# Which pairs of hidden chunks use seven half products, and where the factors of x are made

## The chip, the cores and the metric

The kernel runs on one core of a Trainium2 chip. The metric is the device time of one execution in microseconds (us); lower is better. The engines are TensorE (PE, with its weight loads PEld), VectorE (DVE), ScalarE (ACT), GpSimd (POOL) and SyncE (SP, which issues the DMAs).

## The reference, cut to what matters

```python
x = attention(q, k, v)                  # chunks of 64, as 2304 tokens x 512
x = (x @ w_a) * (x @ w_b) @ w_out       # 512 -> 1536 -> 512
p = probs / probs.sum(-1)
for e in range(4):                      # 512 -> 1024 -> 512
    out += p[:, e:e+1] * (relu(x @ w1[e]) @ w2[e])
```

The change is in the second line. Everything is float32, and each product is made as three matmuls of a value cut into a high and a low part: high by low, high by high, low by high.

## The kernel before, in words

**Tiles.** The 2304 tokens are 18 tiles of 128, in blocks 0 (256 tokens) and 1 to 4 (512 tokens each). The 1536 hidden columns are 12 chunks of 128, in six pairs F = 0 to 5. For a chunk and a block there are a = x @ w_a and b = x @ w_b (12 matmuls each), their product, and the output product, which adds into the accumulator of the block.

**Two forms.** In the plain form (`ab_steps`, L478) a chunk and a block take eight steps of three matmuls. After the last one DVE multiplies (L502), ACT writes the high part (L94, to `gh`), and POOL the low part (L109, to `ag`). The output product (`x2_steps`, L510) of a block and a pair is four steps of six matmuls (three for each chunk; lines L445 to L447), and each ends with an addition to the accumulator (`xacc`, by ACT for pair 0, else by DVE). It is put between steps of the next block: the list `after` says behind which.
In the other form (`seq_ab`, L727) blocks 1 and 2 are made together with a pair of chunks by two sequences of seven half products in place of eight (L614; six matmuls at L605 each). It needs sums of the weights, S1 to S4 (`sums`, L268: four DVE subtractions or additions of 256 columns; `ent_s`, L272, called twice per sequence: a high part on ACT, a low part on POOL, tile `S`), and four factors of x, T1 to T4, which are differences of x's blocks 1 and 2. `first_combos` (L666) makes the factors in 16 steps: `whole` (L675) adds a high and a low part again, `minus` (L695) subtracts, and a split makes a high part on ACT and a low part on POOL or DVE (tile `cT`, at L109 and L101). T1 takes the place of a part of block 2's x, so it can only be made when no plain product of block 2 follows.

**Weights.** A pair has six pieces: a of both chunks, b of both, out of both. `begin_f32` (L263) takes one from 64-bit to 32-bit floats: two ACT operations (L144, L145), three of DVE (L146, L147, L150), one of POOL (L158), then the DMA of a later piece. `prep_end` (L254) splits it: high on ACT, low on POOL (tile `w`).

**Order.** All engines work through their instructions in the order in which the program writes them. That order is written out by hand: `put(u, s, ...)` sets an operation behind step s of block u (in pair 0: behind step s of span u of the list `spans`; "A" is `seq_ab`). Pair 0 runs beside the attention, and its spans 9 and 10 are block 4. Then pair 1 runs blocks 3, 4, 0 and then "A"; pairs 2 to 4 run 4, "A", 3, 0; pair 5 runs "A", 3, 4, 0. The second layer (L830, with half products too) follows and takes the rest of the time.

Of the kernel before, what the change touches and what calls it, by code (L numbers as in the profile page):

```python
# [28 lines left out]
def fused_kernel(  # L29
# [29 lines left out]
    NP1 = w1p.shape[0] // 2  # L59
# [107 lines left out]
    def split_w(src, t=None):  # L167
        t = w_tile() if t is None else t
        split_hi(t[:, 0, :], src)
        sub_hi(nc.gpsimd, t[:, 1, :], src, t[:, 0, :])  # L170
        return t
# [37 lines left out]
    def w_sums(a11, a12, a21, a22):  # L209

        s23 = cv_p.tile([P, 512], F32, tag="t", name="s23", bufs=4)
        s14 = cv_p.tile([P, 512], F32, tag="t", name="s14", bufs=4)
        s2, s3 = s23[:, :256], s23[:, 256:]
        s1, s4 = s14[:, :256], s14[:, 256:]
        add_sb(s1, a21, a22)
        add_sb(s3, a11, a21, ALU.subtract)
        add_sb(s2, s1, a11, ALU.subtract)
        add_sb(s4, a12, s2, ALU.subtract)
        return s23, s14
# [28 lines left out]
    def prep_begin(n=1):  # L248
        for _ in range(n):
            key = pieces[nxt["begin"]]  # L250
            nxt["begin"] += 1
            ready[key] = from_f64(raws[key].pop(0))
# [10 lines left out]
    def begin_f32(F, i):  # L263

        prep_begin()
        f32s[F, i] = ready[0, 2 * F + i % 2, i // 2]

    def sums(F, m):  # L268
        a1, a2 = f32s[F, 2 * m], f32s[F, 2 * m + 1]
        f32s[F, "s", m] = w_sums(a1[:, :256], a1[:, 256:], a2[:, :256], a2[:, 256:])  # L270

    def ent_s(F, m, i):  # L272

        t = late["mid"].tile([P, 2, 512], F32R, tag="S", name="S", bufs=2)
        split_w(f32s[F, "s", m][i], t)
        for x, name in enumerate((("S2", "S3"), ("S1", "S4"))[i]):
            wts["s", F, m, name] = tuple(t[:, h, 256 * x : 256 * x + 256] for h in range(2))
# [313 lines left out]
    def in_place(x1, x2):  # L591
        q = quarters(x1, x2)
        return combos(*q, (q[0], q[1], q[2], q[2]))

    def in_turn(c):
        s1, s2, s3 = c["sums"]
        return c["first"] + s1 + c["T3"] + s2 + c["T2"] + s3 + c["T1"] + c["T4"] + c["B22"]
# [250 lines left out]
    with tc.manual_schedule():  # L848
# [55 lines left out]
        def put(u, s, *go):  # L904
            T.setdefault((u, s), []).extend(go)
# [1 line left out]
        put(6, 3, lambda: begin_f32(1, 0))  # L907
        put(6, 6, prep_end)
        put(7, 3, lambda: begin_f32(1, 1))
        put(8, 7, lambda: sums(1, 0))  # L910
        put(9, 1, lambda: begin_f32(1, 2))
        put(9, 4, prep_end)
        put(9, 5, lambda: ent_s(1, 0, 0))
        put(9, 7, lambda: ent_s(1, 0, 1))
        put(10, 1, prep_end)
        put(10, 2, lambda: begin_f32(1, 3))
        put(10, 6, lambda: sums(1, 1))
        cx = first_combos()
        for i in (5, 7):
            put(10, i, cx.pop(0))  # L920
        x2 = []
        for r, (f, j, i0, nt) in enumerate(spans):
            steps = list(ab_steps(f, j, i0, nt))
# [22 lines left out]
        for F in range(1, NP1):  # L946
            T = {}
            end = F == NP1 - 1
            if F == 1:
                put(3, 8, prep_end)  # L950
                put(3, 9, lambda: begin_f32(F, 4))
                put(3, 10, lambda: begin_f32(F, 5))
                put(3, 13, prep_end)
                put(3, 15, prep_end)
                at = [(3, 5), (3, 11), (3, 13), (4, 1), (4, 3), (4, 4), (4, 6), (4, 8), (4, 10), (4, 12)]
                at += [(4, 14), (0, 2), (0, 5), (0, 7)]
                for (u, s), go in zip(at, cx, strict=True):
                    put(u, s, go)
            else:
                if F == 2:  # L960
                    put(4, 0, lambda: begin_f32(F, 3))
                    put(4, 1, prep_end)
                    put(4, 3, lambda: ent_s(F, 0, 0))
                    put(4, 5, prep_end)
                    put(4, 7, lambda: ent_s(F, 0, 1))
                    put(4, 8, lambda: sums(F, 1))
                    put(4, 9, lambda: begin_f32(F, 4))
                    put(4, 11, lambda: begin_f32(F, 5))
                    put(4, 13, prep_end)
                    put("A", 0, prep_end)  # L970
                else:
                    u = "A" if end else 4
                    put(u, 0, lambda: begin_f32(F, 4))
                    put(u, 8 if end else 2, lambda: begin_f32(F, 5))
                    put(u, 3, prep_end)
                    put(u, 10, prep_end)
            put("A", 4, lambda: ent_s(F, 1, 0))
            put("A", 7, lambda: ent_s(F, 1, 1))
            if not end:
                n = F + 1  # L980
            if F == 1:
                put("A", 6, lambda: begin_f32(n, 0))
                put("A", 8, lambda: begin_f32(n, 1), prep_end)
                put("A", 11, prep_end)
                put("A", 13, lambda: sums(n, 0), lambda: begin_f32(n, 2))
            elif not end:
                put("A", 6, lambda: begin_f32(n, 0))
                put("A", 8, lambda: begin_f32(n, 1))
                put("A", 10, prep_end)
                put(3, 0, lambda: sums(n, 0))  # L990
                put(3, 3, lambda: ent_s(n, 0, 0))
                put(3, 5, lambda: ent_s(n, 0, 1))
                put(3, 14, lambda: begin_f32(n, 2))
                put(0, 4, prep_end)
                put(0, 6, lambda: begin_f32(n, 3))
                put(0, 8, prep_end)
                put(0, 11, lambda: sums(n, 1))
                put(0, 12, prep_end)
            else:
                w_next = w2_steps(0, True)  # L1000
                for u, s in ((4, 3), (0, 4), (0, 8), (0, 12)):
                    put(u, s, lambda: w_next.pop(0)())
                at = [(3, 11 + i) for i in range(4)] + [(3, 15), (4, 0), (4, 2), (4, 4), (4, 6)]
                at += [(4, 8), (4, 10), (4, 12), (4, 14), (4, 15)] + [(0, 2 * i + 1) for i in range(4)]
            for j in ("A", 3, 4, 0) if end else (3, 4, 0, "A") if F == 1 else (4, "A", 3, 0):
                if j == "A":
                    steps = seq_ab(F)
                    after = [4, 5, 6, 7]
                else:
                    nt = blocks[j][1]  # L1010
                    s0, s1 = (list(ab_steps(f, j, 0, nt)) for f in (2 * F, 2 * F + 1))
                    steps = s0[:4] + s1[:4] + s0[4:] + s1[4:]
                    if len(x2) > 4:
                        after = [6 + i for i in range(8)]
                    elif j == 0:
                        after = [8 + 2 * i for i in range(4)]
                    elif (F, j) == (1, 3):
                        after = [4 + i for i in range(4)]
                    else:
                        after = [5 + i for i in range(4)]  # L1020
                if end and j == 3:
                    place = dict(B11="s1", B21="s2", T3="s3", T2="s4", T1="s5", T4="s6", B22="s7")
                    for (u, s), go in zip(at, in_turn(in_place(acc[1], acc[2])), strict=True):
                        put(u, s, go)
                for s, step in enumerate(steps):
                    step()
                    for i, go in enumerate(x2):
                        if after[i] == s:
                            go()
                    for go in T.get((j, s), ()):  # L1030
                        go()
                fs = (2 * F, 2 * F + 1)
                x2 = [x for i in ((1, 2) if j == "A" else (j,)) for x in x2_steps(fs, i, 0, blocks[i][1])]
                if end and j == "A":
                    mid.close()
                    late["p"] = ctx.enter_context(tc.tile_pool(name="late", bufs=1))
# [3 lines left out]
        for p, (j1, j2) in enumerate(((1, 2), (3, 4))):  # L1040
            for g in range(NG2):
                end = p == 1 and g == NG2 - 1
# [97 lines left out]
```

## Time and profile before

| | us |
|---|---|
| runs before | 1270.72, 1270.89, 1272.07 |
| median | 1270.89 |
| the profiled execution | 1272.2 |
| its span, first to last instruction | 1270.4 |

1.8 us of the profiled execution lie around its span. Busy shares are of the span. A matmul's record lasts longer than the time until the next one starts, since matmuls overlap; the time that one takes of the whole is from start to start.

### The profile page before, as it was taken

To read this page: it belongs to the slowest core of one execution; us is meant where nothing else is said; L and a number is where in the kernel's file an instruction comes from. 1 tells how busy PE (TensorE), PEld (TensorE's weight loads), DVE (VectorE), ACT (ScalarE), POOL (GpSimd) and SP (SyncE) were. 2 spreads that over 40 slices of the span, in tenths; PEclk is the share of its full clock that TensorE was granted. 3 is DMA by queue.
4 is the path that set the end of the run, shared out by engine and by line. 5 is a ranking of instruction groups with operands and counts; after the bars stand their busy time and mean duration, and the time that the engine had idled before them with its cause. 6 is when DMAs were issued, how large, how long until landed. Compare 5 with 4: busy or idle time off the path is not lost.

```text
span 1270.4 us, 17613 instructions
## 1 busy us (share of the span) xinstructions
PE 1244.1 (98%) x6856; PEld 1035.2 (81%) x6856; DVE 776.5 (61%) x1233; ACT 451.4 (36%) x746; POOL 374.3 (29%) x290
## 2 busy tenths in 40 slices
PE   8999889899999999999999999999999999999998
PEld 5887768688888888888888888888888888888887
DVE  7865366666665665666566555665575555555555
ACT  4644332423323332322222222222264444444442
POOL 4523544645434553533332323223230000000000
PEclk9999989999999999999999999999999999999999
DMA  7621111212111110234544354534575454544443
GB/s 255 233 90 42 34 33 34 67 34 67 34 34 51 33 50 1 100 134 152 196 156 160 133 189 159 182 133 147 217 249 166 152 163 150 164 152 148 166 133 132
DMA packets 48035, 156.37 MB, mean 123 GB/s; under 512 B 5456, under 2 KB 5456, under 8 KB 47952
## 3 DMA queue, kind: packets, MB, share of 16 engines
q1 hardware_dynamic: 47952, 155.25, 36.7%
q8 instruction: 54, 0.88, 0.3%
q14 instruction: 29, 0.24, 0.1%
HBM read 100.18 MB, written 55.05 MB: 122 GB/s over the span
## 4 chain that ended last, share of the span: by engine, by line
PE 86%; DVE 6%; issue 2%; ACT 2%; POOL 2%; DMA 1%; SPq 0%; POOLq 0%; DVEq 0%; ACTq 0%
PE ps L830 29%; PE pm L605 28%; PE pm L492 11%; PE ps L445 5%; PE ps L447 5%; PE ps L446 5%; PE ps L605 2%; DMA kept<-kept 1%; POOL w L109 1%; PE ps L391 1%; DVE s L101 1%; DVE d L326 1%; DVE mx L325 1%; DVE t L147 1%; POOL ag L109 1%
## 5 line engine op out<-in xcount | busy, mean ns | idle before, releaser
L830 PE MATMUL ps<-w,h 128*128 128x512 f32 x1536 | 353.4, 389 | 0.0
L830 PEld LDWEIGHTS ps<-w,h 128*128 128x128 f32 x1536 | 288.3, 188 | 59.7
L817 DVE SCALAR_TENSOR_TENSOR oacc<-ps,pr,oacc 128x512 f32<-128x512 f32 x270 | 191.7, 749 | 104.4 <-PE ps L830 104.4
L605 PE MATMUL pm<-cT,w 128*128 128x512 f32 x768 | 184.9, 389 | 0.0
L605 PE MATMUL pm<-cB,w 128*128 128x512 f32 x696 | 177.6, 390 | 2.3 <-ACT ag L630 2.0
L605 PEld LDWEIGHTS pm<-cT,w 128*128 128x128 f32 x768 | 144.0, 188 | 29.8
L605 PEld LDWEIGHTS pm<-cB,w 128*128 128x128 f32 x696 | 129.1, 188 | 29.2 <-ACT ag L630 2.9
L109 POOL TENSOR_TENSOR w<-raw,w 128x512 fp32r<-128x512 f32 x64 | 82.7, 1293 | 206.1 <-ACT w L94 142.2
L492 PE MATMUL pm<-xh,w 128*128 128x512 f32 (+1 forms) x576 | 137.2, 359 | 2.8 <-ACT w L94 2.8
L198 ACT CAST w<-kept 128x1024 fp32r<-128x1024 f32 x96 | 99.0, 1046 | 58.9 <-DMA kept<-kept 57.6
L492 PEld LDWEIGHTS pm<-xh,w 128*128 128x128 f32 x576 | 100.3, 192 | 19.9 <-ACT w L94 3.2
L97 DVE TENSOR_TENSOR xacc<-ps,xacc 128x512 f32<-128x512 f32 (+1 forms) x112 | 69.5, 631 | 73.4 <-PE ps L447 73.0
L109 POOL TENSOR_TENSOR ag<-ag,gh 128x512 fp32r<-128x512 f32 (+1 forms) x61 | 78.1, 1286 | 123.1 <-ACT gh L94 121.7
L445 PE MATMUL ps<-ag,w 128*128 128x512 f32 (+1 forms) x244 | 91.8, 376 | 8.9 <-POOL ag L109 8.5
L94 ACT CAST gh<-ag 128x512 fp32r<-128x512 f32 (+1 forms) x61 | 34.9, 572 | 179.5 <-DVE ag L97 143.5
L447 PE MATMUL ps<-gh,w 128*128 128x512 f32 (+1 forms) x244 | 90.8, 372 | 2.3 <-POOL w L109 2.3
L446 PE MATMUL ps<-gh,w 128*128 128x512 f32 (+1 forms) x244 | 90.7, 372 | 0.0
L158 POOL TENSOR_TENSOR t<-t,raw 128x512 int32<-128x512 int32 x36 | 48.0, 1332 | 94.5 <-PE ps L445 31.7
L492 PE MATMUL pm<-xl,w 128*128 128x512 f32 (+1 forms) x288 | 71.8, 361 | 1.4 <-DVE xl L101 1.4
L109 POOL TENSOR_TENSOR w<-s,w 128x512 fp32r<-128x512 f32 x32 | 43.7, 1385 | 72.9 <-ACT w L94 72.9
L97 DVE TENSOR_TENSOR ag<-pm,ag 128x512 f32<-128x512 f32 (+1 forms) x61 | 38.2, 626 | 42.1 <-PE pm L492 26.4
L445 PEld LDWEIGHTS ps<-ag,w 128*128 128x128 f32 x244 | 46.9, 192 | 20.0 <-POOL ag L109 11.1
(122 smaller groups left out, 1686.1 us busy)
## 6 DMA issues: line engine op xcount, KB each, us to landing
kept<-w SPq DMA_DIRECT2D x96, 512.0 KB, 6.1
kept<-kept SPq DMA_DIRECT2D x96, 512.0 KB, 3.3
raw<-in_w1p_dram SPq DMA_DIRECT2D x36, 512.0 KB, 3.6
raw<-in_w2p_dram SPq DMA_DIRECT2D x32, 512.0 KB, 4.5
q<-in_q_dram SPq DMA_DIRECT2D x18, 256.0 KB, 4.5
k<-in_k_dram SPq DMA_DIRECT2D x18, 256.0 KB, 4.7
v<-in_v_dram SPq DMA_DIRECT2D x18, 256.0 KB, 4.5
out_dram<-oacc SPq DMA_DIRECT2D x18, 256.0 KB, 2.6
```

The costliest lines, as they stand in the source:

```text
L94: nc.scalar.copy(out=dst, in_=src)
L97: nc.vector.tensor_tensor(out=out, in0=in0, in1=in1, op=op)
L109: eng.tensor_tensor(out=dst, in0=src, in1=hi.bitcast(F32), op=ALU.subtract)
L158: nc.gpsimd.tensor_tensor(out=t.bitcast(I32), in0=t.bitcast(I32), in1=low.bitcast(I32), op=ALU.add)
L198: nc.scalar.copy(out=t, in_=fetched.pop(key))
L445: nc.tensor.matmul(out=ps[:, :n], lhsT=wh, rhs=al, start=(m == 0), stop=False)
L446: nc.tensor.matmul(out=ps[:, :n], lhsT=wh, rhs=ah, start=False, stop=False)
L447: nc.tensor.matmul(out=ps[:, :n], lhsT=wl, rhs=ah, start=False, stop=(m == last))
L492: nc.tensor.matmul(out=st[i][:, :n], lhsT=x, rhs=y, start=m == 0, stop=m == 3 * KD - 1)
L605: nc.tensor.matmul(out=ps, lhsT=x, rhs=y, start=first and kk == 0 and m == 0, stop=kk == 1 and m == 2, skip_group_check=not first,)
L817: nc.vector.scalar_tensor_tensor(out=o, in0=ps, scalar=p1, in1=o, op0=ALU.mult, op1=ALU.add)
L830: nc.tensor.matmul(out=ps[k], lhsT=x[:, s], rhs=y, start=f == 0 and m == 0, stop=f == 1 and m == 2,)
```

## The change

Pair 1 makes blocks 1 and 2 in the plain form, in the order 1, 2, 3, 4, 0, and has no "A". So the weight sums of pair 1 (`sums(1, ...)`, `ent_s(1, ...)`) are gone, and the 16 steps of the factors, of which two stood in the last span of pair 0 and 14 in blocks 3, 4 and 0 of pair 1, stand in blocks 2, 3, 4 and at the start of block 0, one at a time. The weights of pair 2 are begun in blocks 4 and 0 of pair 1 and no longer in its "A". In pairs 2 to 4 the output product of block 0 of the pair before stands three steps later in block 4, and the out weights are begun and split later; `sums(F, 1)` moves from block 0 of the pair before to step 2 of block 4, but for pair 5.

```diff
         put(7, 3, lambda: begin_f32(1, 1))
-        put(8, 7, lambda: sums(1, 0))
         put(9, 1, lambda: begin_f32(1, 2))
         put(9, 4, prep_end)
-        put(9, 5, lambda: ent_s(1, 0, 0))
-        put(9, 7, lambda: ent_s(1, 0, 1))
         put(10, 1, prep_end)
         put(10, 2, lambda: begin_f32(1, 3))
-        put(10, 6, lambda: sums(1, 1))
-        cx = first_combos()
-        for i in (5, 7):
-            put(10, i, cx.pop(0))
...
             if F == 1:
-                put(3, 8, prep_end)
-                put(3, 9, lambda: begin_f32(F, 4))
-                put(3, 10, lambda: begin_f32(F, 5))
-                put(3, 13, prep_end)
-                put(3, 15, prep_end)
-                at = [(3, 5), (3, 11), (3, 13), (4, 1), (4, 3), (4, 4), (4, 6), (4, 8), (4, 10), (4, 12)]
-                at += [(4, 14), (0, 2), (0, 5), (0, 7)]
-                for (u, s), go in zip(at, cx, strict=True):
+                put(1, 8, prep_end)
+                put(1, 9, lambda: begin_f32(F, 4))
+                put(1, 10, lambda: begin_f32(F, 5))
+                put(1, 13, prep_end)
+                put(1, 15, prep_end)
+                at = [(2, 0), (2, 3), (2, 8), (2, 11), (2, 14), (3, 0), (3, 4), (3, 6), (3, 9), (3, 12)]
+                at += [(3, 14), (4, 3), (4, 5), (4, 11), (4, 14), (0, 1)]
+                for (u, s), go in zip(at, first_combos(), strict=True):
                     put(u, s, go)
             else:
-                if F == 2:
-                    put(4, 0, lambda: begin_f32(F, 3))
-                    put(4, 1, prep_end)
-                    put(4, 3, lambda: ent_s(F, 0, 0))
-                    put(4, 5, prep_end)
-                    put(4, 7, lambda: ent_s(F, 0, 1))
-                    put(4, 8, lambda: sums(F, 1))
-                    put(4, 9, lambda: begin_f32(F, 4))
-                    put(4, 11, lambda: begin_f32(F, 5))
-                    put(4, 13, prep_end)
-                    put("A", 0, prep_end)
-                else:
-                    u = "A" if end else 4
-                    put(u, 0, lambda: begin_f32(F, 4))
-                    put(u, 8 if end else 2, lambda: begin_f32(F, 5))
-                    put(u, 3, prep_end)
-                    put(u, 10, prep_end)
-            put("A", 4, lambda: ent_s(F, 1, 0))
-            put("A", 7, lambda: ent_s(F, 1, 1))
+                u = "A" if end else 4
+                if not end:
+                    put(4, 2, lambda: sums(F, 1))
+                put(u, 0 if end else 4, lambda: begin_f32(F, 4))
+                put(u, 8 if end else 6, lambda: begin_f32(F, 5))
+                put(u, 3 if end else 8, prep_end)
+                put(u, 10 if end else 13, prep_end)
+                put("A", 4, lambda: ent_s(F, 1, 0))
+                put("A", 7, lambda: ent_s(F, 1, 1))
...
             if F == 1:
-                put("A", 6, lambda: begin_f32(n, 0))
-                put("A", 8, lambda: begin_f32(n, 1), prep_end)
-                put("A", 11, prep_end)
-                put("A", 13, lambda: sums(n, 0), lambda: begin_f32(n, 2))
+                put(4, 1, lambda: begin_f32(n, 0))
+                put(4, 7, lambda: begin_f32(n, 1))
+                put(4, 9, prep_end)
+                put(4, 13, lambda: sums(n, 0))
+                put(4, 15, lambda: ent_s(n, 0, 0))
+                put(0, 2, lambda: ent_s(n, 0, 1))
+                put(0, 3, lambda: begin_f32(n, 2))
...
+            if not end:
                 put(0, 4, prep_end)
                 put(0, 6, lambda: begin_f32(n, 3))
                 put(0, 8, prep_end)
-                put(0, 11, lambda: sums(n, 1))
+                if n == NP1 - 1:
+                    put(0, 11, lambda: sums(n, 1))
                 put(0, 12, prep_end)
...
-            for j in ("A", 3, 4, 0) if end else (3, 4, 0, "A") if F == 1 else (4, "A", 3, 0):
+            for j in ("A", 3, 4, 0) if end else (1, 2, 3, 4, 0) if F == 1 else (4, "A", 3, 0):
...
-                    elif (F, j) == (1, 3):
+                    elif F > 1 and j == 4 and not end:
+                        after = [8 + i for i in range(4)]
+                    elif j == 1:
                         after = [4 + i for i in range(4)]
```

## Rows read from the trace of the kernel before

**Rows 1.** The page: busy time of each engine over the span.
```profile
PE 1244.1 (98%) x6856; PEld 1035.2 (81%) x6856; DVE 776.5 (61%) x1233; ACT 451.4 (36%) x746; POOL 374.3 (29%) x290
```
**Rows 2.** What TensorE waited for: total us, times, longest us.
```profile
PE ps L445 <- POOL ag L109: 8.5, 5, 3.7
PE pm L492 <- ACT w L94: 2.8, 1, 2.8
PE ps L447 <- POOL w L109: 2.3, 2, 1.5
```
**Rows 3.** Pairs 1, 2, 3: length, busy PE, PEld, DVE, ACT, POOL, clock, DMA, GB/s.
```profile
137.10:218.40 81.30, 71.79 (x326) 58.63 (x325) 43.59 (x59) 24.64 (x45) 35.22 (x25) 0.94 0.11 32
218.40:304.20 85.80, 81.38 (x373) 67.50 (x372) 58.32 (x83) 28.17 (x51) 47.88 (x36) 0.98 0.17 51
304.20:375.50 71.30, 71.15 (x347) 59.91 (x346) 43.99 (x67) 22.55 (x41) 33.59 (x27) 1.00 0.15 44
```
**Rows 4.** Timeline of TensorE: start, us, matmuls, [idle before <- releaser].
```profile
122.70 0.50 PE L445 MATMUL ps<-ag,w 128*128 128x512 f32 x1 [0.88 <-POOL ag L109]
...
145.08 0.71 PE L445 MATMUL ps<-ag,w 128*128 128x512 f32 x1 [3.71 <-POOL ag L109]
...
148.83 0.40 PE L445 MATMUL ps<-ag,w 128*128 128x512 f32 x1
...
160.89 1.98 PE L492 MATMUL pm<-xh,w 128*128 128x512 f32 x8
162.70 0.61 PE L492 MATMUL pm<-xl,w 128*128 128x512 f32 x2
...
164.69 0.50 PE L447 MATMUL ps<-gh,w 128*128 128x512 f32 x1 [0.84 <-POOL w L109]
168.09 0.50 PE L445 MATMUL ps<-ag,w 128*128 128x512 f32 x1 [2.91 <-POOL ag L109]
...
170.30 0.80 PE L447 MATMUL ps<-gh,w 128*128 128x512 f32 x1 [1.47 <-POOL w L109]
...
175.98 0.40 PE L445 MATMUL ps<-ag,w 128*128 128x512 f32 x1
...
188.85 0.50 PE L445 MATMUL ps<-ag,w 128*128 128x512 f32 x1 [0.58 <-POOL ag L109]
...
229.47 0.96 PE L492 MATMUL pm<-xh,w 128*128 128x512 f32 x3 [2.81 <-ACT w L94]
...
233.87 0.43 PE L445 MATMUL ps<-ag,w 128*128 128x512 f32 x1
...
249.30 1.65 PE L605 MATMUL pm<-cB,w 128*128 128x512 f32 x6 [1.61 <-ACT ag L630]
```
**Rows 5.** Timeline of GpSimd around the first two boundaries of pair 1.
```profile
138.62 2.40 POOL L677 TENSOR_TENSOR tmp<-cB 128x1024 f32<-128x1024 f32 x1
...
160.40 1.31 POOL L158 TENSOR_TENSOR t<-t,raw 128x512 int32<-128x512 int32 x1 [1.24 <-DVE t L150]
161.66 1.30 POOL L109 TENSOR_TENSOR ag<-ag,gh 128x512 fp32r<-128x512 f32 x1
163.07 1.56 POOL L109 TENSOR_TENSOR w<-t,w 128x512 fp32r<-128x512 f32 x1
```
**Rows 6.** Timeline of VectorE, alone and at the same two boundaries.
```profile
120.43 0.76 DVE L101 SCALAR_TENSOR_TENSOR s<-t 128x256 f32<-128x256 f32 x2
...
138.70 2.94 DVE L101 SCALAR_TENSOR_TENSOR s<-t 128x256 f32<-128x256 f32 x2 [1.57 <-POOL t L158]
...
160.09 0.69 DVE L97 TENSOR_TENSOR ag<-pm,ag 128x512 f32<-128x512 f32 x1
161.98 3.20 DVE L101 SCALAR_TENSOR_TENSOR cT<-tmp,cT 128x512 fp32r<-128x512 f32 x2 [1.21 <-ACT cT L94]
165.11 0.68 DVE L97 TENSOR_TENSOR ag<-pm,ag 128x512 f32<-128x512 f32 x1
```
**Rows 7.** Timeline of ScalarE at the second boundary.
```profile
160.81 0.62 ACT L94 CAST gh<-ag 128x512 fp32r<-128x512 f32 x1 [3.21 <-DVE ag L97]
```

More of the change, by code (lines that the diff above doesn't have):

```diff
@@ L996, in fused_kernel @@
                 put(0, 8, prep_end)
-                put(0, 11, lambda: sums(n, 1))
+                if n == NP1 - 1:
+                    put(0, 11, lambda: sums(n, 1))
                 put(0, 12, prep_end)
-            else:
+            if end:
                 w_next = w2_steps(0, True)
```

## The prediction

> **What bounds the kernel now.** The page first: TensorE is busy for 1244.1 of 1270.4 us [rows 1], and no other engine comes near. So a change pays either by fewer matmuls or by taking a wait of TensorE away. This one adds matmuls; the question is which waits it takes. The table of waits names them: TensorE waits for low parts that POOL makes of the gated product (8.5 us) and of weights (2.3), and for a weight's high part (2.8) [rows 2]. The stretches tell where: pair 1 has 71.79 busy us in 81.30 at a granted clock of 0.94, pair 2 has 81.38 in 85.80 at 0.98, pair 3 has 71.15 in 71.30 at 1.00 [rows 3]. So the waits, and the clock's falls behind them, lie in pairs 1 and 2, which the change rewrites, and pair 3 shows the same kind of work without any.
>
> **The waits priced.** Undisturbed, eight matmuls of 512 columns take 162.70 - 160.89 = 1.81 us, 0.227 each [rows 4]. A wait costs 0.16 more than its bracket (a matmul's own 0.39 outlasts the 0.227 by that), and the first matmul behind it some 0.11 more (0.50 for 0.39). I name them by place.
> - A, output products of block 3 in the last spans of pair 0: 0.88 + 0.27 = 1.15.
> - B, output product of block 4 in pair 1's first block: 3.71 + 0.16, and then nine matmuls from 145.08 to 148.83 take 3.75 instead of 9 x 0.227 = 2.04, at the lower of the two clock levels (1.2 for 2.4 GHz): 5.58.
> - C, the next boundary: 0.84 + 2.91 + 1.47 + 3 x 0.16, and 13 matmuls from 170.30 to 175.98 take 5.68 for 2.95: 8.43, with two slow first matmuls 8.7.
> - D, into block 0: 0.58 + 0.27 = 0.85.
> - E, pair 2's block 4 for the split of its second a piece: 2.81 + 0.16, and 12 matmuls from 229.47 to 233.87 take 4.40 for 2.72: 4.65.
> - F, in pair 2's "A": 1.61 + 0.27 = 1.88.
> Together 22.8 us [rows 4].
>
> **What is added.** Two blocks times two chunks times 24 matmuls are 96; the two sequences have 84. So 12 more, 12 x 0.227 = 2.72 us, with nothing to hide them. Everything else of TensorE's work stays.
>
> **What is removed or moved, by its place.**
> *Last spans of pair 0 and B.* B's chain: the sums of the second two pieces stand on DVE ahead of the last product. Two of their four operations took 2.94 us, where a pair alone takes 0.76 [rows 6], beside a `whole` on POOL of 2.40 [rows 5]. Sums, `whole` and weight parts leave this place. DVE, ACT and POOL then need 0.69, 0.62 and 1.30 [rows 5 to 7] behind the last matmul, 2.6 us and small hand-overs; the second chunk's low part is wanted five steps (15 x 0.227 = 3.4) and three matmuls later, at 4.1. B goes to 0. A has the same chain of 2.6 with the same two steps before it; it loses at most its lengthened POOL operation: 1.05 stays.
> *C.* Now the first boundary inside pair 1 is from block 1 to block 2, with the same conversions of the two out pieces at the same steps (8, 9, 10, 13, 15), but without factor steps between. Up to the product of the first chunk nothing changes: DVE at 160.09 [rows 6], ACT at 160.81 [rows 7], POOL at 161.66, since POOL's conversion of the second out piece ran from 160.40 [rows 5]. What goes is T3 on DVE (3.20 for two), which held the second chunk's product back from 160.8 to 165.11 [rows 6]. POOL then works through its queue at 1.30 each: first low part until 162.96, first out weight until 164.3, second low part until 165.6, second out weight until 166.9. TensorE wants them at 162.70 + 2 x 0.227 = 163.15 [rows 4], 163.6, 163.8 and 164.3: it waits some 0.7, 1.0 and 0.9, in all 2.6 us instead of the 5.7 before. Does the clock fall? Bounds: 0, as at F, whose single 1.61 us left it high, and 2.7, as at C now. The longest single piece is like F, the sum like E, where 1.7 was lost. I take 1.4, near E, since over half of that stretch is idle.
> *Blocks 2 to 4.* Two `whole` (2.40 each [rows 5]) queue on POOL behind the out weights of C, until about 172, before block 2's first product. T3's low part comes ahead of block 2's second product on DVE: two operations of 512 columns, 0.76 each if twice a single one of 256, or 1.60 each beside POOL [rows 6], so the second low part is done within 0.3 us of when it is wanted. T1's low part (2.5 on POOL) falls behind block 3's output products and is done before its first product. I take 0.2 for both; bounds 0 and one `whole`, 2.4.
> *D.* On DVE, T4's two differences (1.5 by the same reckoning) and pair 2's sums (four operations, 0.38 each alone [rows 6]) now stand ahead of block 4's second product, where before there was one addition. With one wait for POOL's low part of the first chunk (1.3) they end some 1.6 us after the last matmul, about a quarter of a microsecond later than now: 1.1 instead of 0.85. Bounds: 0 and 2.4. The rows of DVE beside POOL show each lengthened by about one POOL operation [rows 5, 6]. The Trainium skill's SBUF - State Buffer, section Who interferes with whom, says that a VectorE instruction with two SBUF inputs and a GpSimd one that reads SBUF shut each other out for a whole instruction; the trace agrees (2.94 for two beside 2.40). By that rule two of these six could each wait for a different POOL instruction, and D would be 2.4, the sum 1.3 us less gain.
> *Block 0 and pair 2's block 4 (E).* The piece that E waits for is now begun at step 7 of block 4 and split in block 0 at step 4, a whole block before it is used: E goes to 0. But POOL gets a pile in block 0: two S, T4 (two), two conversions, three weights, 10 x 1.30, two half-width low parts of 0.74 and block 4's last 1.30: 15.8 us, against 11 us of matmuls there (48 of 256 columns, taken at half of 0.227, and 24 of 512). The output product of block 0 has been set back to step 8 of pair 2's block 4, nine steps of three matmuls, 6.1 us, more. It just fits; the DVE operations in between push it over by 0.5. Bounds: 0 and 3.
> *F and later.* Pair 2 now has the order of pair 3, which has no wait [rows 3]: F goes to 0. In pairs 3 and 4, `sums` on DVE and the out weights only move within block 4, where POOL has six operations (7.8 us) in some 13.6 us (48 matmuls of 512 columns and 24 of 256): 0, or a boundary of 0.85 as at D if that cover is gone. The DMAs move with the conversions that issue them, two pieces ahead on a queue that carries nothing else there (SP): 0, or one wait like F's (1.9).
>
> **The sum.** Left over: A 1.05, C 2.6 + 1.4, blocks 2 to 4 0.2, D 1.1, block 0 0.5: 6.85. Gain 22.8 - 6.85 - 2.72 = 13.2 us. The profiled execution took 1272.2, so it would take 1259.0; the median of the runs is 1.3 lower, 1270.9, and gives 1257.7. I forecast 1257.5.
>
> **Rivals.**
> 1. *All waits go* but A (C's chain overlaps, the pile fits): gain 22.8 - 1.05 - 2.72 = 19.0, 1252. For it: pair 3 has none. Against: C's chain is POOL's own queue, five operations in a row that the change leaves. 0.13.
> 2. *DVE and POOL hold each other up* wherever factor steps stand beside low parts, by the rule named at D. D 2.4, block 0 3 us and a fall of the clock like E's 1.7: 4.4 + 1.1 more than in my sum is 5.5 less gain, 1263. For it: each of the three long DVE rows stands beside POOL [rows 5, 6]. Against: they are now spread over five blocks. 0.19.
> 3. *The conversions, not the factors, make C and E*, so that the change doesn't do what it says: C stays at 8.7 and E at 4.65: gain 3.8, 1267. For it: C waits for out weights twice [rows 4]. Against: at C, DVE's second product stands behind T3 in the rows, and E's piece is now a block earlier. 0.09.
> 4. *Slower*: POOL's long factor steps push the second low part at each of the four boundaries, 1 to 2, 2 to 3, 3 to 4 and 4 to 0, as far as at C now: 4 x 8.7 + 1.15 + 2.72 = 38.7 against 22.8, 16 slower, 1287. It decides from (22.8 - 1.15 - 2.72) / 4 = 4.7 us a boundary. For it: C's size. Against: only `whole` and T1, T4 are on POOL, and each stands where its block's low parts are done or not begun. 0.04.
>
> **How the numbers follow.** The forecast has 0.55; its own range is 1254 to 1261 (the clock at C 0 to 2.7, block 0 from 0 to 2). The range reaches over rival 1 and most of rival 2: 1251.5 to 1265.5. A measurement of this kernel can tell 0.2%, 2.5 us. Faster by more: the forecast, rivals 1 and 2 and nearly all of 3, 0.94. Within: 0.03, where 3 and 4 shade into no change. Slower: 0.03.
>
> **What would show it.** Pair 1 with a clock near 1.00 and at most 5 us idle; no wait of over 1 us at the start of pair 1's first block; a broken wait of 2 to 3 us for POOL's `ag` and `w` in block 2; about 1 us into block 0; pair 2 as clean as pair 3 but for its first output product; 12 more matmuls in all. Waits of over 3 us for `ag` at several boundaries would make it wrong, and so would a new wait for T in pair 2's "A".

## The result, and the profile after

The kernel after takes 1257.41 us (median of 4 runs, 1256.42 to 1258.08) against 1271.1 of the kernel before (a fourth run, 1271.3, stands beside the three given above): a ratio of 0.9891, interval 0.9873 to 0.9908. The profiled executions stand at 1258.08 and 1272.2 us, spans 1256.3 and 1270.4. So 14.1 us of the profiled time are to be found.

The page of the kernel after, busy time as in [rows 1]:

```profile
PE 1239.7 (99%) x6868; PEld 1032.7 (82%) x6868; DVE 762.6 (61%) x1215; ACT 449.7 (36%) x743; POOL 367.5 (29%) x286
```

There are 12 matmuls more, and 18 DVE, 3 ACT and 4 POOL instructions fewer. The stretches of pairs 1 and 2, columns as in [rows 3]:

```profile
137.10:214.00 76.90, 74.76 (x345) 61.51 (x344) 40.82 (x52) 27.78 (x50) 35.59 (x26) 1.00 0.12 35
214.00:290.50 76.50, 75.56 (x371) 63.89 (x370) 51.70 (x76) 24.26 (x44) 43.21 (x33) 1.00 0.18 56
```

Pair 1 is idle for 2.1 us where it was for 9.5, pair 2 for 0.9 where it was for 4.4, and the granted clock is 1.00 in both instead of 0.94 and 0.98. All waits of TensorE that are left from the last spans of pair 0 to the end of pair 2, in its timeline:

```profile
123.05 0.50 PE L445 MATMUL ps<-ag,w 128*128 128x512 f32 x1 [0.76 <-POOL ag L109]
...
158.90 0.49 PE L447 MATMUL ps<-gh,w 128*128 128x512 f32 x1 [0.39 <-POOL w L109]
160.13 0.50 PE L445 MATMUL ps<-ag,w 128*128 128x512 f32 x1 [0.73 <-POOL ag L109]
161.36 0.50 PE L447 MATMUL ps<-gh,w 128*128 128x512 f32 x1 [0.49 <-POOL w L109]
...
209.86 0.50 PE L445 MATMUL ps<-ag,w 128*128 128x512 f32 x1 [0.53 <-POOL ag L109]
...
224.91 0.39 PE L445 MATMUL ps<-ag,w 128*128 128x256 f32 x1 [0.94 <-POOL ag L109]
```

Priced as the prediction prices them (each bracket, the idle time before a matmul, with 0.27 for what the first matmul behind it takes longer):

| place | before | foreseen | after |
|---|---|---|---|
| A, last spans of pair 0 | 1.15 | 1.05 | 1.03 |
| B, first block of pair 1 | 5.6 | 0 | 0 |
| C, second block (block 2) | 8.7 | 2.6 + 1.4 for the clock | 2.4, the clock stays |
| blocks 2 to 4 | - | 0.2 | 0 |
| D, into block 0 | 0.85 | 1.1 | 0.80 |
| first output product in pair 2 | - | 0.5 | 1.2 |
| E, pair 2's block 4 | 4.65 | 0 | 0 |
| F, pair 2's "A" | 1.9 | 0 | 0 |

That is 22.8 us before and 5.5 after. With 2.7 for the matmuls, 14.6 go; and the kernel after comes to wait A 0.5 later than the one before (123.05 less its 0.76, against 122.70 less 0.88 in [rows 4]). That half microsecond lies in the attention: already the first product of the second line starts at 22.02 instead of 21.52, where both kernels have run the same instructions. 14.1 remain, as measured. The same without prices: from the first matmul of pair 1 to the first of pair 3 it takes 152.35 us where it took 167.11, 14.8 less.

### The profile page after: what moved, and what is told of

Read it like the earlier page. It is cut to its first block, busy times and chain, and to the rows that moved or that the text cites. A ratio compares the mean times of both kernels' runs of the same rounds, so it can differ in the third digit from the quotient of the medians.

```text
span 1256.3 us, 17592 instructions
## 1 busy us (share of the span) xinstructions
PE 1239.7 (99%) x6868; PEld 1032.7 (82%) x6868; DVE 762.6 (61%) x1215; ACT 449.7 (36%) x743; POOL 367.5 (29%) x286
## 4 chain that ended last, share of the span: by engine, by line
PE 90%; DVE 5%; ACT 2%; issue 1%; POOL 1%; DVEq 0%; POOLq 0%; ACTq 0%
PE ps L830 31%; PE pm L605 28%; PE pm L492 13%; PE ps L445 5%; PE ps L447 5%; PE ps L446 5%; PE ps L605 2%; DVE d L326 1%; DVE mx L325 1%; DVE t L147 1%; DVE raw L146 1%; PE ps L391 1%; DVE cB L101 0%; PE ps L116 0%; POOL ag L109 0%
## 5 line engine op out<-in xcount | busy, mean ns | idle before, releaser
L605 PE MATMUL pm<-cB,w 128*128 128x512 f32 x672 | 171.2, 390 | 1.0 <-ACT m L630 0.7
L605 PEld LDWEIGHTS pm<-cB,w 128*128 128x128 f32 x672 | 124.8, 188 | 26.7 <-POOL cT L109 1.1
L492 PE MATMUL pm<-xh,w 128*128 128x512 f32 (+1 forms) x576 | 134.6, 355 | 0.0
L97 DVE TENSOR_TENSOR xacc<-ps,xacc 128x512 f32<-128x512 f32 (+1 forms) x112 | 69.9, 631 | 76.4 <-PE ps L447 75.8
L447 PE MATMUL ps<-gh,w 128*128 128x512 f32 (+1 forms) x244 | 89.2, 366 | 0.9 <-POOL w L109 0.9
L446 PE MATMUL ps<-gh,w 128*128 128x512 f32 (+1 forms) x244 | 89.2, 366 | 0.0
L97 DVE TENSOR_TENSOR ag<-pm,ag 128x512 f32<-128x512 f32 (+1 forms) x61 | 38.1, 626 | 42.8 <-PE pm L492 30.7
L97 DVE TENSOR_TENSOR u<-pm,m 128x512 f32<-128x512 f32 x32 | 22.1, 692 | 62.0 <-PE pm L605 62.0
```

Source lines behind the costliest of these rows:

```text
L97: nc.vector.tensor_tensor(out=out, in0=in0, in1=in1, op=op)
L446: nc.tensor.matmul(out=ps[:, :n], lhsT=wh, rhs=ah, start=False, stop=False)
L447: nc.tensor.matmul(out=ps[:, :n], lhsT=wl, rhs=ah, start=False, stop=(m == last))
L492: nc.tensor.matmul(out=st[i][:, :n], lhsT=x, rhs=y, start=m == 0, stop=m == 3 * KD - 1)
L605: nc.tensor.matmul(out=ps, lhsT=x, rhs=y, start=first and kk == 0 and m == 0, stop=kk == 1 and m == 2, skip_group_check=not first,)
```

## The experiments

The theory: every wait in pairs 1 and 2 is for an operation (a low part; at E and F one of ACT's) that comes late because something stands ahead of it, in the order of its engine, on DVE or POOL, or ahead of what it waits for; so the gain is one of place. The rival: the gain is one of form; the half products made the waits, and only the plain blocks leave room beside them. Medians are given with their ratio to the kernel before, run beside each.

**Both parts of B put back** (`e1`, on the kernel after; the sums are computed and not used)

```diff
+        put(10, 6, lambda: sums(1, 1))
+        cx = first_combos()
+        for i in (5, 7):
+            put(10, i, cx.pop(0))
...
-                at = [(2, 0), (2, 3), (2, 8),
+                at = [(2, 8),
...
```

> The kernel after, with the weight sums of pair 1's out-side pieces (unused here) and the first two factor steps (whole) put back into the last span of pair 0. Theory (place): what stands ahead of block 4's last gated product makes wait B. B comes back at 4 to 5.6 us, with the lower clock level behind it, all later places stay as in the kernel after: about 1262 us. Rival (form): the waits came from the half products of pair 1, which are still gone: B stays at 0 and the time within 1 us of 1257.4.

Measured: 1262.65 us, 0.9931 (0.9918 to 0.9945). **Each part alone** (`e5`, the first line; `e6`, the others):

> The kernel after with only the weight sums (unused) back in the last span of pair 0. Theory: on DVE alone they end 1.6 us behind POOL's conversion, and the product, its high and its low part follow: B is 1.5 to 1.8 us and the clock stays. Port theory: most of B's 3.8 in the run with both came from DVE's sums and POOL's whole shutting each other out, so the two parts alone give less together than both did. Rival: the sums alone make it all, 3.5 us or more.

> The kernel after with only the first two whole steps back in the last span of pair 0. Theory: POOL's 2.4 us stand ahead of the second low part and leave B at 0.9 to 1.3 us, the clock stays. Port theory: less than 3.8 together with the run that has the sums alone. Rival: whole alone makes it all, 3.5 us or more.

Measured, in one run each: 1259.13 and 1259.09 us. Rows of TensorE, VectorE and GpSimd in the run with both:

```profile
144.79 0.50 PE L445 MATMUL ps<-ag,w 128*128 128x512 f32 x1 [3.62 <-POOL ag L109]
...
138.42 2.94 DVE L101 SCALAR_TENSOR_TENSOR s<-t 128x256 f32<-128x256 f32 x2 [1.47 <-POOL t L158]
...
138.34 2.39 POOL L677 TENSOR_TENSOR tmp<-cB 128x1024 f32<-128x1024 f32 x1
```

In the run with the sums alone:

```profile
142.51 0.50 PE L445 MATMUL ps<-ag,w 128*128 128x512 f32 x1 [1.45 <-POOL ag L109]
...
138.31 0.76 DVE L101 SCALAR_TENSOR_TENSOR s<-t 128x256 f32<-128x256 f32 x2 [1.47 <-POOL t L158]
```

In the run with `whole` alone:

```profile
142.68 0.50 PE L445 MATMUL ps<-ag,w 128*128 128x512 f32 x1 [0.84 <-POOL ag L109]
...
139.00 2.40 POOL L677 TENSOR_TENSOR tmp<-cB 128x1024 f32<-128x1024 f32 x1
```

B returns without a half product in pair 1: there the theory of place holds and the rival falls. From the first matmul of pair 1 to that of pair 2 the kernel after takes 79.81 us, with the sums alone 81.61, with `whole` alone 80.95, with both 85.34. That is 1.8, 1.1 and 5.5 more; the priced wait is 1.7, 1.1 and 3.9 of it, and the last 1.6 are the lower clock that only the longer wait brought on. So 1.1 us of the wait is there only with both. It can be followed: the sums alone leave 1.45, and the same two DVE operations take 2.94 beside `whole` where they take 0.76 alone, 2.18 more. Together 3.63; measured 3.62. So beside the sums `whole` costs by holding DVE and not by its own place in POOL's queue, which alone left 0.84.

**Place without form** (`e2`, on the kernel before)

```diff
-        put(10, 6, lambda: sums(1, 1))
-        cx = first_combos()
-        for i in (5, 7):
-            put(10, i, cx.pop(0))
...
-                at = [(3, 5), (3, 11), (3, 13), (4, 1), (4, 3), (4, 4), (4, 6), (4, 8), (4, 10), (4, 12)]
-                at += [(4, 14), (0, 2), (0, 5), (0, 7)]
+                put(3, 3, lambda: sums(1, 1))
+                at = [(3, 4), (3, 6), (3, 7), (4, 0), (4, 5), (4, 6), (4, 7), (4, 7), (4, 9), (4, 9), (4, 10)]
+                at += [(4, 12), (4, 14), (0, 2), (0, 5), (0, 7)]
...
```

> The kernel before, seven half products in pair 1 and no matmul more, with the weight sums, the two whole steps and the T3 steps only set later, into pair 1's blocks 3 and 4. Theory (place): B goes to 0 and C shrinks from 8.7 to the 2.4 that POOL's conversions leave; D, E and F stay at 0.9, 4.7 and 1.9: 11.9 us less than before, about 1259. Rival (form): without the plain blocks there is not enough time beside them, so what leaves B and C comes back in blocks 4 and 0 or in A: 1265 or more.

Measured: 1262.26 us, 0.9928 (0.9916 to 0.994), between the theory's 1259 and the rival's 1265. The waits left at C, D and E in its timeline of TensorE:

```profile
158.15 0.50 PE L447 MATMUL ps<-gh,w 128*128 128x512 f32 x1 [0.49 <-POOL w L109]
159.37 0.51 PE L445 MATMUL ps<-ag,w 128*128 128x512 f32 x1 [0.73 <-POOL ag L109]
160.61 0.50 PE L447 MATMUL ps<-gh,w 128*128 128x512 f32 x1 [0.50 <-POOL w L109]
179.30 0.50 PE L445 MATMUL ps<-ag,w 128*128 128x512 f32 x1 [1.78 <-POOL ag L109]
219.97 1.65 PE L492 MATMUL pm<-xh,w 128*128 128x512 f32 x3 [2.80 <-ACT w L94]
```

B is gone and C is the wait of the kernel after, for seven half products and no matmul more. D has more than doubled (2.05), so a part came back there, and E and F are untouched (2.80; 1.61 as before). Place alone gives 8.8 of the 13.7 us.

**E taken too, with half products** (`e11`, on the version above; `e12` adds moves like those of `e9` below, sets pair 1's sums from step 3 to step 10 of block 3, and six of the factor steps up to three steps later)

```diff
-                    put(4, 1, prep_end)
...
-                put("A", 6, lambda: begin_f32(n, 0))
-                put("A", 8, lambda: begin_f32(n, 1), prep_end)
+                put("A", 0, lambda: begin_f32(n, 0))
+                put("A", 2, lambda: begin_f32(n, 1))
+                put("A", 8, prep_end)
+                put("A", 9, lambda: sums(n, 0))
+                put("A", 10, lambda: begin_f32(n, 2))
                 put("A", 11, prep_end)
-                put("A", 13, lambda: sums(n, 0), lambda: begin_f32(n, 2))
+                put("A", 13, prep_end)
```

> The spread version of the kernel before (seven half products in pair 1), with pair 2's first pieces begun at steps 0 and 2 of pair 1's A instead of 6 and 8, its sums at step 9 instead of 13, and its third piece begun at step 10 and split at step 13 instead of in pair 2. Theory (place): E waits for that third piece, which stands behind the sums; E goes from 4.7 (6.0 with the longer fall of the clock in the spread run) to 0, the rest stays: 1256.3 to 1257.6. Rival (form): A leaves DVE and POOL no room, so E stays above 2 us or a wait as large opens in A: 1260 or more.

> The same, with the out pieces of pair 1 converted early in block 3, its second sums behind step 10 there, the last steps of T2 and T4 behind block 4's last product, and the output product of block 3 one step later in the next-to-last span of pair 0: the moves of the version with all moves, without the plain blocks. Theory (place): A 0.4, C and D under 0.5 each, B, E 0, F stays at 1.9: 1251 to 1252.5, with 12 matmuls less than the version with all moves (1252.0). Rival (form): the plain blocks are needed to hold these steps; waits of 4 us or more are left in pairs 1 and 2: 1254 or more.

Measured: 1263.02 us, 0.992 (0.9907 to 0.9934), and 1261.0, 0.9913 (0.99 to 0.9927): both come out where the rival put them, at 1260 or more and at 1254 or more. Their runs scatter by 4.5 and 3.6 us, more than those of the other versions. The run `e11`, TensorE and VectorE inside pair 1's "A":

```profile
210.24 2.72 PE L605 MATMUL pm<-cB,S 128*128 128x512 f32 x6 [2.02 <-DVE gh L97]
...
205.91 1.39 DVE L101 SCALAR_TENSOR_TENSOR s<-t,s 128x256 f32<-128x256 f32 x1
207.23 0.68 DVE L97 TENSOR_TENSOR gh<-pm,gh 128x512 f32<-128x512 f32 x1
...
208.90 0.69 DVE L150 SCALAR_TENSOR_TENSOR t<-t,raw 128x512 uint32<-128x512 uint32 x1
209.51 0.68 DVE L97 TENSOR_TENSOR gh<-pm,gh 128x512 f32<-128x512 f32 x1
```

E is gone, and a new wait stands in "A": the last half product adds into the bank that DVE's L97 at 209.51 has yet to read. Ahead of it in DVE's order stands the conversion of the third piece (its last operation is the L150), which began only when the sums, ahead of both, were done. In `e12` the same 2.01 is there. B, D and E are gone in it too, but a wait of 4.09 stands at C, where its sums stand ahead of the products, and ahead of them a `minus` of 2.30, for which DVE sat idle for 7.42 us until POOL's `whole` was done:

```profile
160.60 0.63 PE L445 MATMUL ps<-ag,w 128*128 128x512 f32 x1 [4.09 <-POOL ag L109]
...
153.09 2.30 DVE L101 SCALAR_TENSOR_TENSOR tmp<-tmp 128x1024 f32<-128x1024 f32 x1 [7.42 <-POOL tmp L677]
155.31 1.84 DVE L101 SCALAR_TENSOR_TENSOR s<-t 128x256 f32<-128x256 f32 x2
```

Here the rival has its part. In "A" TensorE wants DVE's result one or two half products later, in the plain form a low part some 4 us later; so the sums and a conversion cost 2 us beside the one, and the sums 0.8 beside the other (D in the kernel after). But each new wait stands behind something that these two orders put there. Whether another order would carry E and C with half products stays open, and with it how much of the change's last 4.9 us needs the plain form.

**What is left of C, D and in pair 2** (`e3`, `e7`, `e8`, and `e4` the other way, each on the kernel after)

```diff
-                put(1, 8, prep_end)
-                put(1, 9, lambda: begin_f32(F, 4))
-                put(1, 10, lambda: begin_f32(F, 5))
-                put(1, 13, prep_end)
-                put(1, 15, prep_end)
+                put(1, 1, lambda: begin_f32(F, 4))
+                put(1, 5, lambda: begin_f32(F, 5))
+                put(1, 6, prep_end)
+                put(1, 8, prep_end)
+                put(1, 9, prep_end)
```

> The kernel after, with the two out pieces of pair 1 converted behind steps 1 and 5 of block 1 instead of 9 and 10, and the three splits behind steps 6, 8 and 9. Theory: what is left of C is POOL's queue of two conversions, two low parts and two weights in a row, so with the conversions out of it C goes from 2.4 to under 0.3: about 1255.0. Rival: C's rest is the chain product, high part, low part of the second chunk itself: it stays above 1.5 and the time within 1 us of 1257.4.

Measured: 1255.06 us, 0.9874 (0.986 to 0.9887). Its stretch over the first four blocks of pair 1, columns as in [rows 3], has no idle time:

```profile
135.00:205.00 70.00, 70.00 (x321) 58.43 (x320) 37.92 (x50) 23.42 (x42) 31.14 (x22) 1.00 0.13 38
```

So C's rest was POOL's queue, as the prediction lists it.

```diff
-                put(4, 13, lambda: sums(n, 0))
-                put(4, 15, lambda: ent_s(n, 0, 0))
+                put(0, 0, lambda: sums(n, 0))
+                put(0, 1, lambda: ent_s(n, 0, 0))
```

> The kernel after with pair 2's first weight sums moved from step 13 of block 4 to step 0 of block 0, behind block 4's last product, and the first split to step 1. Theory: the sums on DVE ahead of the product make wait D; without them D goes from 0.8 to under 0.2, and the 1.2 us wait of pair 2's first output product changes by at most half a us either way: 1256.0 to 1257.2. Rival: D is the chain of product, high and low part, and stays at 0.8.

Measured: 1255.93 us, 0.9877 (0.9862 to 0.9891). D is gone. The time is just under the range expected. The only wait from there to the end of pair 2 is

```profile
222.97 0.39 PE L445 MATMUL ps<-ag,w 128*128 128x256 f32 x1 [0.55 <-POOL ag L109]
```

Then `after = [8 + i ...]` of block 4 becomes 10 (`e8`) or 5 (`e4`):

> The kernel after with the output product of block 0 set two steps later still (10 for 8) in block 4 of pairs 2 to 4. Theory: wanted 1.4 us later, the low part that POOL's pile delays is there: the 1.2 us wait of pair 2 goes to 0, nothing else changes, 1256.2. Rival: the later output product delays the next one's additions or buffers and a wait of its size shows up behind it: 1257.4 or more.

> The kernel after, with the output product of block 0 put back to step 5 of the next pair's block 4 (from step 8) in pairs 2 to 4. Theory: POOL's pile of block 0 is what its first matmul waits for in pair 2; wanted 2.0 us sooner, its 1.2 grows to 3.2, with the clock's fall up to 5, and nothing happens in pairs 3 and 4, where there is no pile: 1259.5 to 1261. Rival: the wait follows the step and not POOL's pile: it stays at 1.2 and the time at 1257.4.

Measured: 1256.79 us, 0.9882 (0.9865 to 0.9898), between the theory's 1256.2 and the rival's 1257.4, and in the profile the wait is gone; and 1261.18, 0.9917 (0.9902 to 0.9933), where it is two:

```profile
224.14 0.39 PE L445 MATMUL ps<-ag,w 128*128 128x256 f32 x1 [1.00 <-POOL ag L109]
226.42 0.39 PE L445 MATMUL ps<-ag,w 128*128 128x256 f32 x1 [1.66 <-POOL ag L109]
```

So it is POOL's pile that the product waits for. Setting the product back by three steps is worth 3.5 us of the change by the profiles (pair 2 takes 76.07 us in `e4` and 72.54 in the kernel after, each from its first matmul to pair 3's) and 3.8 by the medians; the prediction has it only as what just makes room for the pile.

**All moves together** (`e9`: those of `e3`, `e7`, `e8`, and `steps.insert(2 * i + (3 if r == 9 else 2), go)` for A; `e10`: the kernel after again, beside it)

> The kernel after with the three moves together (out pieces of pair 1 converted early, pair 2's first sums behind block 4's last product, output product of block 0 at step 10) and the output product of block 3 one step later in the next-to-last span of pair 0. Theory: the waits left in the kernel after are each a low part that comes behind something on DVE or POOL, so they add up: C 2.4, D 0.8 and pair 2's first output product 1.2 go, and A falls from 1.04 to 0.4: 5.1 us less than 1257.4, 1252.3. Rival: what is moved out of one place lands in the next; under 3 us in all, 1254.5 or more.

> The kernel after once more, beside the one with all moves on the same chip: 1257.4 within 0.8 us. Where the broken wait in block 2 is followed by a fall of the clock, 1.5 us more than where it is not, so a spread of about 1.5 us among its runs.

Measured: 1251.99 us, 0.9852 (0.9836 to 0.9869), and 1257.92 (1257.35 to 1258.51, so the spread is 1.2 and not 1.5), 0.9894 (0.9879 to 0.9909). The four waits are gone, A but for 0.4, so the moves add up and this version is the fastest of those run.

## Why the prediction was right

**The waits priced, and where they went.** B, C, E and F went to what was said, and C's broken wait has the three pieces foreseen (0.7, 1.0, 0.9; measured 0.39, 0.73 and 0.49, or 2.4 with what surrounds them), for the reason given: with POOL's conversions moved out it vanishes. The sum left was 6.85 and is 5.5; the profiled time foreseen was 1259.0 and is 1258.1, since 0.5 of the 1.4 less went into the later start.

F went as said, but no run tries it by itself. By its rows it is of the same kind: before, DVE converts pair 2's second out piece (its last operation is the L150) ahead of two additions and the gated product, and ACT's copy, for which TensorE waits at F, stands behind that product's high part:

```profile
245.62 0.69 DVE L150 SCALAR_TENSOR_TENSOR t<-t,raw 128x512 uint32<-128x512 uint32 x1
246.23 1.28 DVE L97 TENSOR_TENSOR xacc<-ps,xacc 128x512 f32<-128x512 f32 x2
247.43 0.68 DVE L97 TENSOR_TENSOR ag<-pm,ag 128x512 f32<-128x512 f32 x1
...
248.67 0.58 ACT L630 COPY ag<-pm 128x512 f32<-128x512 f32 x1
```

In the kernel after this piece begins at step 6 of block 4 and no longer at step 11: in pair 2 the out weights come sooner, and only in pairs 3 and 4 later.

**Mis-sized.** The clock at C: 1.4 taken, 0 in this profile. The first output product of pair 2: 0.5 taken, 1.2 measured. The prediction counts ten full POOL operations in the pile, but its own list has nine (two S, two of T4, two conversions, three weights), so 14.5 us and not 15.8, which would have fitted. In the trace POOL is busy for 15.56 us there (columns as in [rows 3]), since some of its operations took longer than 1.30, and sits idle once, for 0.78, until DVE has converted a piece:

```profile
208.52:224.86 16.34, 14.92 (x76) 12.27 (x75) 14.44 (x15) 7.19 (x15) 15.56 (x12) 1.00 0.22 66
...
211.01 2.93 POOL L109 TENSOR_TENSOR cT<-ag,cT 128x512 fp32r<-128x512 f32 x2
...
219.30 1.31 POOL L158 TENSOR_TENSOR t<-t,raw 128x512 int32<-128x512 int32 x1 [0.78 <-DVE t L150]
```

So one operation too many hid most of what the two engines cost each other here. DVE's conversions beside the pile took up to 3.6 times as long. Two of the same kind, in the pile and 11 us later:

```profile
214.41 1.52 DVE L146 TENSOR_SCALAR raw<-raw 128x512 uint32<-128x512 uint32 x1
...
225.52 0.42 DVE L146 TENSOR_SCALAR raw<-raw 128x512 uint32<-128x512 uint32 x1
```

D: 1.1 taken, 0.80 measured; the sums' first two operations waited once (1.86 below), as reckoned, and the second two not at all:

```profile
204.53 1.86 DVE L101 SCALAR_TENSOR_TENSOR s<-t 128x256 f32<-128x256 f32 x2
206.32 0.41 DVE L101 SCALAR_TENSOR_TENSOR s<-s,t 128x256 f32<-128x256 f32 x1
```

These three, with 0.2 more at C and the 0.2 for blocks 2 to 4, leave the sum 1.4 too high. That the median, 1257.41, lies within 0.1 of the forecast is luck: the later start gave back 0.5, the profiled run lies 0.7 above the median where the prediction took 1.3, and the forecast is 0.2 under its own sum.

**Misnamed.** The prediction has E wait for "the split of its second a piece". By the order it is the first b piece, wanted at step 8 of block 4, begun at step 13 of "A" behind the sums and split at step 1 of block 4. `e11` began this piece three steps sooner and split it inside "A", and E went. It moved the two pieces before it and the sums as well. The price and the conclusion stand; the reason given for it (begun at step 7 of block 4) was of another piece: this one is now begun at step 3 of block 0 and split at step 8 there.

**The rivals.** The first, all waits gone, is what `e9` reaches by four more moves. The second, DVE and POOL holding each other up, has its mechanism shown (0.76 against 2.94) but not its size here: D 0.8 and not 2.4, the first output product 1.2 and not 3, and no fall of the clock. The Trainium skill's SBUF - State Buffer, section Who interferes with whom, has the rule that a VectorE instruction with two SBUF inputs contends with a GpSimd one that reads SBUF, and the trace agrees (0.76 against 2.94). The third, that the conversions make C and E, is right for 2.4 of C's 8.7. The fourth, four boundaries as bad as C, did not come: blocks 2 to 4 have no wait. That 12 matmuls cost 2.7 us was not tried by itself; the account closes with it.

## What to carry to other kernels

When every engine works in a written order, price a wait by following the one late instruction back through its engine's queue, and ask of each thing ahead of it whether its own deadline is later. A form with more matmuls can win (here 2.7 us of them beside 17 us less waiting) if it gives the side engines deadlines 4 us away instead of one or two products. Before changing the form, try the places: they gave 8.8 of 13.7 us here, and four more moves behind the change gave another 5.9.

## What was not expected of the hardware

**The clock's fall is not settled by the wait alone.** With the same broken wait at C (brackets within 0.1), the stretch behind it ran at the full clock in the kernel after (1.00) and mostly at the lower of the two levels in `e4` (0.55 over the stretch), columns as in [rows 3]; first the kernel after:

```profile
161.70:165.50 3.80, 3.80 (x18) 3.15 (x17) 1.39 (x2) 0.59 (x1) 3.80 (x2) 1.00 0.00 0
```

Then `e4`:

```profile
161.70:165.50 3.80, 3.80 (x11) 3.00 (x10) 0.70 (x2) 0.00 (x0) 3.80 (x2) 0.55 0.00 0
```

Of the ten profiles that have this wait, it fell in two (`e4` and `e2`). Where it fell it cost 1.6 us (pair 1 takes 81.44 us in `e4` and 79.81 in the kernel after). So the prediction's 1.4 was near the price of a fall, and mostly none came. A wait in one piece is no surer: D has a bracket of 1.78 in `e2` and of 1.77 in `e11`. The stretch behind it in `e2`, and then in `e11`:

```profile
181.00:183.50 2.50, 2.50 (x15) 2.12 (x15) 1.02 (x2) 0.02 (x1) 0.75 (x1) 1.00 0.03 7
...
180.00:182.50 2.50, 2.50 (x7) 1.96 (x7) 0.09 (x1) 0.00 (x0) 0.82 (x1) 0.50 0.00 0
```

**Who starts first decides which engine pays.** At the end of pair 5 a wait of 0.9 us for a low part (`yl`) is in `e3`, `e4`, `e8` and `e11` and not in the kernel after, though nothing was changed near. In the kernel after DVE starts 0.07 us ahead of POOL, and POOL's operation is long:

```profile
516.25 1.22 POOL L109 TENSOR_TENSOR yl<-xacc,yh 128x256 fp32r<-128x256 f32 x1
...
516.18 0.68 DVE L771 SCALAR_TENSOR_TENSOR h<-m,h 128x512 fp32r<-128x512 f32 x1
```

In `e3` POOL starts 0.02 ahead, and DVE's is, with TensorE's wait a few operations behind it:

```profile
513.29 0.75 POOL L109 TENSOR_TENSOR yl<-xacc,yh 128x256 fp32r<-128x256 f32 x1
...
513.31 1.27 DVE L771 SCALAR_TENSOR_TENSOR h<-m,h 128x512 fp32r<-128x512 f32 x1
```

It goes so in every profile of this case: POOL starts first by 0.01 to 0.03 us in the four that have the wait, and DVE by up to 0.16 in the ten that have not. What decides between them is not shown; with nothing changed near, a wait of 0.9 us can come with a change far away.
